# A retention layer and a swish MLP in one kernel: when TensorE gets the hosted batch's outputs and crosses, which PSUM bank its states take, and how the last rows are stored

## The chip, the cores and the metric

One core of one Trainium2 chip runs the kernel. The metric is the device time of the whole program in microseconds (us). The kernel before took 297.31 us, the median of three runs (296.36 to 298.05).

## The reference

Eight batches of eight heads (S = 576 positions, head width 64) go through a causal retention: scores of q and k, each multiplied by gamma(head) to the power of the distance, then multiplied by v. The result, 4608 rows of 512, goes through `g = h * sigmoid(beta * h)` with `h = x @ w_in` (512 to 2048), and `g @ w_out` (2048 to 512) is returned in float32.

```
ret = scale * (q @ k^T) * gamma ** (i - j)   for i >= j, else 0
x   = (ret @ v), heads side by side          # 4608 x 512
h   = x @ w_in ; g = h * sigmoid(beta * h)   # 4608 x 2048
out = g @ w_out                              # 4608 x 512
```

## The kernel before, in words

**Tiling.** Each batch's first 512 positions are one block of rows; the last 64 positions of all eight batches together are a ninth block. Blocks are counted 0 to 8 here. For every block, TensorE makes 16 "ups" (`up`, L702: four matmuls of 128x512 into one PSUM bank, which ScalarE then turns into `gT`), and then the second matrix product. Blocks 0 to 2 do that product directly (`down`, L806). From block 3 on it is done with seven products in the manner of Strassen (`seven_mm`, L739, in the order 3, 4, 1, 5, 2, 7, 6): each is 16 matmuls of 128x256, on the halves of `gT` itself or on sums of such halves (`seven_a`, L723, on VectorE), against combinations of w_out's quarters that were made before (`seven_b`, L248 and L244). In these blocks the odd rows of `gT` take two steps: ScalarE writes `hs` (L706) and VectorE scales it into `gT` (L707).

**The hosted batch.** While TensorE works at block n it also does the retention of batch b = n + 1, in small matmuls of 64x64, which run four at a time. Batch b's work has these steps: `scores` (sc and the second half of the batch's states, `four_states`), the folds (`fold`, L533 to L542: VectorE adds each of four partial states to a running sum, the fourth one at L537, and writes bf16 copies), four masks (L286, VectorE, from the scores in PSUM to `R`), `outputs4` (O<-R,vn, needs all four masks), a small copy on ScalarE that orders two kinds of matmul in one bank (`fence`, L505), and `crosses4` (O from q and the earlier states; for most batches also the first half of the next batch's states). Then O is copied into `xT`, the operand of the next block's ups (L625). In block 7 the ninth block's rows take the same place (`tail_scores`, `tail_outputs`, `tail_crosses`).

**PSUM.** Eight banks in rings by tag: `mm` (three: ups, the chains U and W, and one of the two banks of four states), `st` (one: the other bank of four states), `O` and `sc` (two each). A tile of a ring waits for the readers of the tile that held its bank. `state_banks` (L522) gives two banks for four partial states: those with index 0 and 1 lie in bank 0, those with 2 and 3 in bank 1, and `fold` reads them in this order. Before, bank 0 is `st` and bank 1 is `mm`.

**The order.** Nothing is scheduled by a tool: `fill` is TensorE's list (ups, downs, products), and `merged` (L826) puts other steps before the item at which they are due. In the lists `t = base[n]` is the first up of block n, so `t + 14` means ahead of its up 14, and `t + 16` ahead of its first product (two items for each product). All engines get their instructions in the order in which the steps are put, and each engine runs its own in that order. The lines that set the order here are L996 to L1002 (sums for the products) and L1005 to L1036 (hosted batch). For n = 3 (`SB`) outputs4 is due at t + 14 and crosses4 at t + 15; for n = 4, 5, 6 at t + 12 and t + 13; in block 7 at t + 13 and t + 14. In block 1 the second half of the scores is due 9.5 items ahead of block 2's first up, outputs4 4.2 items later and crosses4 one more.

**Loads and stores.** All large DMAs are issued by SP in the same order of steps: loads of q, k and v, transposes (L362), stores. GpSimd casts and scales q, k, v (L317, L328, L354). The products' results are gathered in `ot` and stored by `seven_store` (L768): after product 7 two rows of tiles, after product 6 the other two, 256 KB each.

Of the kernel before, what the change touches and what calls it, by code (L numbers as in the profile page):

```python
# [11 lines left out]
F32 = mybir.dt.float32  # L12
# [7 lines left out]
def kernel(  # L20
# [22 lines left out]
    TL = S - MB  # L43
# [6 lines left out]
    SB = 3  # L50
    KH = FO // 2
    NH = d_model // 2
# [13 lines left out]
    psum = ctx.enter_context(tc.psum_pool(name="psum", bufs=1))  # L66
# [218 lines left out]
    def F(f, *a):  # L285
        return lambda: f(*a)  # L286
# [232 lines left out]
        return [F(step, p, j ^ x) for p in range(HP) for j in range(2)]  # L519

    def state_banks():
        return [psum.tile([P, 2, HP, D], F32, name="st", tag=t, bufs=n) for t, n in (("st", 1), ("mm", 3))]  # L522
# [80 lines left out]
    def crosses4(b, later=None):  # L603
# [140 lines left out]
    def seven_out(m, j, ps, n):  # L744

        if m not in ots:
            ots[m] = stage.tile([P, MB // P, d_model], F32, name="ot", tag="ot", bufs=2)
        q = ots[m][:].rearrange("s (p a) (c n) -> s a c p n", a=2, c=2)
        c11, c12, c21, c22 = (q[:, a, c, ps] for a in range(2) for c in range(2))
        U, W, Z = (chains.get((c, n)) for c in "UWZ")  # L750
        if j == 4:
            nc.scalar.copy(c12, W[:])
            nc.vector.tensor_tensor(c21, c12, U[:], ALU.add)
        elif j == 1:
            nc.scalar.copy(c22, Z[:])
        elif j == 5:
            nc.scalar.copy(c11, W[:])
            nc.vector.tensor_tensor(c12, c21, c11, ALU.subtract)
        elif j == 2:
            nc.vector.tensor_tensor(c21, c21, U[:], ALU.subtract)  # L760
        elif j == 7:
            nc.vector.tensor_tensor(c11, c11, Z[:], ALU.add)
            seven_store(m, 0, ps)
        elif j == 6:
            nc.vector.tensor_tensor(c22, c22, U[:], ALU.add)
            seven_store(m, 1, ps)

    def seven_store(m, a, ps):  # L768

        for p in range(ps.start, ps.stop):  # L770
            if m < B:
                nc.sync.dma_start(out[m * S:m * S + MB].rearrange("(s i) n -> s i n", i=CB)[:, 2 * p + a], ots[m][:, 2 * p + a])
            else:
                rows = out.rearrange("(b s) n -> s b n", s=S)[MB + a * TL // 2:MB + (a + 1) * TL // 2, CB * p:CB * (p + 1)]
                nc.sync.dma_start(rows, ots[m][:, 2 * p + a])

    phs = {}

# [14 lines left out]
    pos_, ots, held = {}, {}, []  # L793
# [117 lines left out]
    base = {1: u1 + 10}  # L911
# [75 lines left out]
    def queued(at, steps):  # L987
        return [(x, lambda: steps.pop(0)()) for x in at]
# [7 lines left out]
    for n in range(SB, B + 1):  # L996
        t, m = base[n], blocks[n]
        first, second = slice(0, KH // 2), slice(KH // 2, KH)
        early = [t + 14.2, t + 14.9, t + 15.6, t + 15.8] if n == SB else [t + 9.6, t + 10.4, t + 11.2, t + 14.4] if n < B else span(t + 9, 4)
        streams.append([(x, F(seven_a, m, j, first)) for x, j in zip(early, (1, 5, 2, 7))] +  # L1000
                       [(t + 16.4 + 0.1 * x, F(seven_a, m, j, second)) for x, j in enumerate((1, 5, 2, 7))] +
                       [(t + 22.1, F(seven_a, m, 6))])  # L1002

    todo = list(range(2 * CB, len(seq), 2))
    for n in range(1, B):  # L1005

        take = [i for i in todo if seq[i][0] == n + 1 or n == B - 1]
        todo = todo[len(take):]
        b, t = n + 1, base[n]
        t0 = t + lead.get(n, 0)  # L1010
        if n == 1:
            at = [t + 17, base[b] - 9.5]
        elif n < SB:
            at = [t + 3, t + 18]
        else:
            at = [t0 - 13, t0 + 2] if n < B - 1 else [t0 - 9.5, t0 - 2.5]
        for i, x in zip(take, at, strict=True):
            streams.append(pair_prep(i, x))
        if n == 1:
            streams.append([(d0 + 6.1, F(mask, late, [1, CB], [CB, PC // 2])),  # L1020
                            (d0 + 6.2, F(mask, tri, [1, TL]))])
            streams.append([(at[0], F(group1, b, (0,))), (at[1], F(group1, b, (1,))), (at[1] + 4.2, F(outputs4, b)), (at[1] + 5.2, F(crosses4, b))])
        elif n < SB:
            streams.append([(t + 16, F(first_states, b))] * (b == XB + 1) +
                           [(t + 19, F(group1, b, (0, 1))), (t + 25, F(outputs4, b)), (t + 26, F(crosses4, b))])
        elif n == B - 1:
            outs = []
            streams.append([(t0, F(tail_scores, take[0])), (t + 13, F(tail_outputs, take[0])), (t + 14, F(tail_crosses, take[0], outs))] +
                           queued([t + 16.3, t + 17.6, t + 20.5, t + 22.5], outs))
        else:  # L1030
            rest, outs = [], []
            t0 -= behind[n]
            if b == SB + 2 and SB == XB + 1:
                streams.append([(t + 0.5, F(first_states, b))])
            streams.append([(t0, F(scores, b, (0, 1), rest))] + queued(span(t0 + 0.1, 4, 0.8) + span(t0 + 3.3, 4, 0.9), rest))
            streams.append([(t + (14 if n == SB else 12), F(outputs4, b)), (t + (15 if n == SB else 13), F(crosses4, b, outs))] + queued([t + 16.3] * 4 + [t + 17.3, t + 18.3, t + 20.3, t + 20.4][:0 if n in (SB, B - 2) else 4], outs))  # L1036
    assert not todo
    merged(fill, *streams)

# [29 lines left out]
```

## Time and profile before

| | |
|---|---|
| time, median of 3 runs | 297.31 us (296.36 to 298.05) |
| profiled execution: its time / its span | 297.5 us / 295.8 us |
| mean granted TensorE clock | 0.999 |
| HBM read / written | 36.71 MB / 9.44 MB, 156 GB/s over the span |
| ACT busy | 170.9 us (58%) |
| POOL busy | 123.3 us (42%) |
| DMA packets | 128309, 54.03 MB |

The span runs from the first to the last instruction; 1.7 us of the profiled time lie outside it. A TensorE matmul's record is longer than the time that it holds the engine, since matmuls are pipelined: the next one starts before the record ends. So time that TensorE lost is read here as the distance from one start to the next, less what the instruction between them usually takes. Times in a timeline row are: start, length (of a run of instructions, if xN is over 1), and in brackets the idle time before it and what ended it.

### The profile page before, as it was taken

How to read it: one execution, taken by the hardware profiler on the slowest of the kernel's cores; microseconds unless marked ns; L12 is line 12 of the kernel's file. 1: busy time of each engine (PE TensorE's matmuls, PEld its weight loads, DVE VectorE, ACT ScalarE, POOL GpSimd, SP SyncE). 2: the span in 40 equal slices, each digit the busy share in tenths (PEclk: the TensorE clock that was granted, in tenths of full speed). 3: DMA queues.
4: the chain of work that ended last, by engine and by line, in shares of the span. 5: the costliest groups of instructions: out<-in, count | busy, mean ns of one | idle time of the engine just before them, and what ended most of it. 6: DMA issues, size and time to landing. Idle time of an engine off the chain costs nothing.

```text
span 295.8 us, 8242 instructions
## 1 busy us (share of the span) xinstructions
PE 282.8 (96%) x3433; PEld 174.1 (59%) x3433; DVE 185.1 (63%) x341; ACT 170.9 (58%) x300; POOL 123.3 (42%) x219
## 2 busy tenths in 40 slices
PE   7799999999899999979999999899999999999994
PEld 5554446864444544437844685468547854784583
DVE  6563556704994395397579854987497645652672
ACT  5577556687858873655156734673376157737730
POOL 5666216673746381496447159245066200000000
PEclk9999999999999999999999999999999999999999
DMA  7999999998999999799798969955588530003003
GB/s 212 218 348 387 386 265 224 234 182 195 217 173 240 237 249 175 186 268 194 132 242 227 194 182 276 189 109 115 179 191 149 91 144 3 2 31 113 0 0 144
DMA packets 128309, 54.03 MB, mean 183 GB/s; under 512 B 110336, under 2 KB 120592, under 8 KB 128272
## 3 DMA queue, kind: packets, MB, share of 16 engines
q1 hardware_dynamic: 128240, 53.49, 78.7%
q8 instruction: 27, 0.44, 0.7%
q14 instruction: 10, 0.08, 0.1%
q10 hardware_dynamic: 32, 0.01, 0.0%
HBM read 36.71 MB, written 9.44 MB: 156 GB/s over the span
## 4 chain that ended last, share of the span: by engine, by line
PE 64%; SPq 14%; DMA 10%; DVE 8%; issue 1%; POOL 1%; ACT 1%; DVEq 0%; POOLq 0%
PE ph L702 27%; PE U L739 11%; SPq L100 8%; PE po L806 8%; PE W L739 7%; PE Z L739 7%; DMA wt<-in_moe_w_out_dram 3%; PE O L499 3%; DMA wt<-in_moe_w_in_dram 2%; DVE gT L707 2%; SPq L105 2%; DMA kvn<-in_v_dram 2%; DVE R L286 2%; PE sc L499 2%; SPq L86 1%; DMA kT<-kn 1%
## 5 line engine op out<-in xcount | busy, mean ns | idle before, releaser
L702 PE MATMUL ph<-xT,w_in_sb 128*128 128x512 bf16 (+1 forms) x560 | 118.7, 364 | 1.6 <-DVE end L537 1.4
L702 PEld LDWEIGHTS <-w_in_sb 128*128 128x128 bf16 x560 | 52.5, 98 | 57.0 <-DVE end L537 2.9
L709 ACT ACTIVATE gT<-ph,beta_sb 128x512 bf16<-128x512 f32 (+1 forms) x92 | 58.3, 641 | 46.6 <-PE ph L702 45.7
L354 POOL CAST kn<-kvn 128x128 bf16<-128x128 f32 (+2 forms) x80 | 32.8, 444 | 55.9 <-DMA kvn<-in_k_dram 55.6
L707 DVE TENSOR_SCALAR gT<-hs,ratio 128x512 bf16<-128x512 f32 x48 | 28.3, 589 | 35.4 <-ACT hs L706 35.1
L739 PEld LDWEIGHTS <-sa 128*128 128x128 bf16 x480 | 47.0, 98 | 5.4
L706 ACT ACTIVATE hs<-ph,beta_sb 128x512 f32<-128x512 f32 x48 | 33.0, 687 | 20.8 <-PE ph L702 20.5
L806 PE MATMUL po<-w_out_sb,gT 128*128 128x512 bf16 x192 | 43.8, 379 | 0.0
L723 DVE TENSOR_TENSOR sa<-gT 128x1024 bf16<-128x1024 bf16 (+1 forms) x54 | 41.5, 807 | 1.5 <-PE Z L739 1.3
L317 POOL TENSOR_TENSOR qs<-qn,gq 128x256 bf16<-128x256 f32 (+1 forms) x36 | 27.6, 792 | 23.4 <-issue 13.0
L328 POOL TENSOR_TENSOR vn<-kvn,gv 128x512 bf16<-128x512 f32 x32 | 34.6, 1090 | 4.4 <-DMA kvn<-in_v_dram 3.2
L806 PEld LDWEIGHTS <-gT 128*128 128x128 bf16 x192 | 17.9, 98 | 20.2
L739 PE MATMUL U<-b,sa 128*128 128x256 bf16 x192 | 22.9, 273 | 0.0
L739 PE MATMUL Z<-b,sa 128*128 128x256 bf16 x192 | 22.9, 273 | 0.0
L286 DVE TENSOR_TENSOR R<-sc,late 128x512 bf16<-128x512 f32 x24 | 15.3, 681 | 11.4 <-issue 10.2
L739 PEld LDWEIGHTS <-gT 128*128 128x128 bf16 x192 | 18.8, 98 | 3.4
L248 DVE TENSOR_TENSOR b<-wt 128x512 bf16<-128x512 f32 x20 | 15.2, 815 | 3.1 <-ACT wt L231 1.8
L407 DVE TENSOR_TENSOR R<-sc,causal 128x512 bf16<-128x512 f32 x16 | 10.2, 685 | 4.6 <-PE sc L403 4.5
L788 PE MATMUL ph<-xT,w_in_sb 128*128 128x512 bf16 x56 | 12.5, 379 | 0.2 <-ACT xT L460 0.2
L739 PE MATMUL U<-b,gT 128*128 128x256 bf16 x96 | 11.5, 273 | 0.0
L739 PE MATMUL W<-b,gT 128*128 128x256 bf16 x96 | 11.5, 273 | 0.0
L739 PE MATMUL W<-b,sa 128*128 128x256 bf16 x96 | 11.5, 273 | 0.0
(119 smaller groups left out, 288.5 us busy)
## 6 DMA issues: line engine op xcount, KB each, us to landing
out_dram<-ot SPq DMA_DIRECT2D x36, 256.0 KB, 3.3
qn<-in_q_dram SPq DMA_DIRECT2D x16, 512.0 KB, 5.5
kvn<-in_k_dram SPq DMA_DIRECT2D x20, 256.0 KB, 5.3
kvn<-in_v_dram SPq DMA_DIRECT2D x20, 256.0 KB, 5.3
wt<-in_moe_w_out_dram SPq DMA_DIRECT2D x8, 512.0 KB, 9.3
kvn<-in_k_dram SPq DMA_DIRECT2D x24, 128.0 KB, 3.6
kvn<-in_v_dram SPq DMA_DIRECT2D x24, 128.0 KB, 3.8
wt<-in_moe_w_in_dram SPq DMA_DIRECT2D x5, 512.0 KB, 8.4
```

The costliest lines, as they stand in the source:

```text
L100: nc.sync.dma_start(t[:, j], src[c * P:(c + 1) * P])
L286: return lambda: f(*a)
L317: nc.gpsimd.tensor_tensor(batch[b]["qs"][:, cs, to], q_tiles[b][:, hs, cs].rearrange("p h i d -> p i h d"), gq[:, cs, hs].unsqueeze(3).to_ ...
L328: nc.gpsimd.tensor_tensor(live[i]["vn"][:], kv_tiles.pop(i)[:, 1], gains(gv, row_of(b, c)), ALU.mult)
L354: nc.gpsimd.tensor_copy(kn[:, c % 2, to], t[:, 0, hs])
L702: nc.tensor.matmul(ph, w_in_sb[:, ko, fo * P:(fo + 1) * P], xts[m][:, ko, :, w], start=(ko == 0), stop=(ko == KO - 1))
L706: nc.scalar.activation(h, ph, ACT.Silu, scale=beta_sb[:, fo:fo + 1])
L707: nc.vector.tensor_scalar(gts[m][:, fo], h, ratio[:, fo // 2:fo // 2 + 1], None, ALU.mult)
L709: nc.scalar.activation(gts[m][:, fo, :, w], ph, ACT.Silu, scale=beta_sb[:, fo:fo + 1])
L723: nc.vector.tensor_tensor(sums_a[0][:, held_in[j], ks], quarter(m, *x, ks), quarter(m, *y, ks), op)
L739: nc.tensor.matmul(chains[c, n][:, 0 if alone else p], a, sevens[k // 2][:, j - 1, k % 2, :], start=j in (3, 4, 1) and k == 0 and (alone o ...
L806: nc.tensor.matmul(po[:, :nn], gT[:, fo, ms, :], w_out_sb[:, fo, n0:n0 + nn], start=(fo == 0), stop=(fo == FO - 1))
```

## The change

It does four things. Each engine keeps the computing instructions that it had; SP has four more stores.

1. `state_banks`: bank 0 of four partial states is now in `mm` and bank 1 in `st`.
2. `outputs4` and `crosses4` get other places: block 3, t + 14 / t + 15 becomes t + 15.3 / t + 17.3 (all 16 ups first, then outputs, product 3, crosses); block 4, t + 12 / t + 13 becomes t + 13 / t + 15.2 (crosses behind all ups); blocks 5 and 6, outputs at t + 10 (two ups sooner), crosses still at t + 13; block 7, outputs two ups sooner; block 2, crosses one item later. In block 1 the second half of the scores comes one item later, outputs stay where they were, and crosses come one item later. Copies of O queued for block 3 come two items later.
3. `seven_a`: in block 3 the sums are put in the order of the products that need them, both halves of the sum for products 1 and 5 ahead of those for 2 and 7; in block 4 the first halves are due at t + 11, 12, 14.4, 15.3 where they were due at t + 9.6, 10.4, 11.2, 14.4; in blocks 5 to 7 two due times move by 0.2 and 0.4, which changes no order on VectorE there.
4. `seven_store`: in the ninth block (m == B) each half row of tiles is stored as soon as its product has finished it, eight stores of 128 KB in place of four of 256 KB. In other blocks nothing changes.

```
-        return [... for t, n in (("st", 1), ("mm", 3))]
+        return [... for t, n in (("mm", 3), ("st", 1))]
...
+            done = (0, slice(NH, d_model))        # after product 5; likewise 2, 7, 6
...
+        if m == B and j in (5, 2, 7, 6):
+            seven_store(m, done[0], ps, done[1])
+        elif m < B and j in (7, 6):
+            seven_store(m, done[0], ps, slice(0, d_model))
...
+        if n == SB:
+            halves = [(t + 14.4, 1, first), (t + 15.1, 5, first), (t + 16.3, 1, second), (t + 16.4, 5, second)] + \
+                     [(t + 17.5 + 0.5 * x, j, ks) for x, (j, ks) in enumerate((j, ks) for j in (2, 7) for ks in (first, second))]
+        else:
+            early = [t + 11, t + 12, t + 14.4, t + 15.3] if n == SB + 1 else [t + 9.6, t + 10.6, t + 11.6, t + 14.4] if n < B else span(t + 9, 4)
...
-            at = [t + 17, base[b] - 9.5]
+            at = [t + 17, base[b] - 8.9]
...
-            ... (at[1] + 4.2, F(outputs4, b)), (at[1] + 5.2, F(crosses4, b))
+            ... (at[1] + 3.9, F(outputs4, b)), (at[1] + 5.9, F(crosses4, b))
...
-                           ... (t + 25, F(outputs4, b)), (t + 26, F(crosses4, b))
+                           ... (t + 25, F(outputs4, b)), (t + 27, F(crosses4, b))
...
-            ... (t + 13, F(tail_outputs, take[0])), (t + 14, F(tail_crosses, take[0], outs))
+            ... (t + 11, F(tail_outputs, take[0])), (t + 14, F(tail_crosses, take[0], outs))
...
-            streams.append([(t + (14 if n == SB else 12), F(outputs4, b)), (t + (15 if n == SB else 13), F(crosses4, b, outs))] + queued([t + 16.3] * 4 + ...
+            by = (t + 15.3, t + 17.3) if n == SB else (t + 13, t + 15.2) if n == SB + 1 else (t + 10, t + 13)
+            streams.append([(by[0], F(outputs4, b)), (by[1], F(crosses4, b, outs))] + queued([t + 16.3 + 2 * (n == SB)] * 4 + ...
```

More of the change, by code (lines that the diff above doesn't have):

```diff
@@ L521, in state_banks @@
     def state_banks():
-        return [psum.tile([P, 2, HP, D], F32, name="st", tag=t, bufs=n) for t, n in (("st", 1), ("mm", 3))]
+        return [psum.tile([P, 2, HP, D], F32, name="st", tag=t, bufs=n) for t, n in (("mm", 3), ("st", 1))]
     def four_states(b, e, bank):
@@ L998 @@
         first, second = slice(0, KH // 2), slice(KH // 2, KH)
-        early = [t + 14.2, t + 14.9, t + 15.6, t + 15.8] if n == SB else [t + 9.6, t + 10.4, t + 11.2, t + 14.4] if n < B else span(t + 9, 4)
-        streams.append([(x, F(seven_a, m, j, first)) for x, j in zip(early, (1, 5, 2, 7))] +
-                       [(t + 16.4 + 0.1 * x, F(seven_a, m, j, second)) for x, j in enumerate((1, 5, 2, 7))] +
+        if n == SB:
[3 more added lines that the diff above has]
+            early = [t + 11, t + 12, t + 14.4, t + 15.3] if n == SB + 1 else [t + 9.6, t + 10.6, t + 11.6, t + 14.4] if n < B else span(t + 9, 4)
+            halves = [(x, j, first) for x, j in zip(early, (1, 5, 2, 7))] + [(t + 16.4 + 0.1 * x, j, second) for x, j in enumerate((1, 5, 2, 7))]
+        streams.append([(x, F(seven_a, m, j, ks)) for x, j, ks in halves] +
                        [(t + 22.1, F(seven_a, m, 6))])
```

21 lines of the change are left out of this document (11 added, 10 removed).

## The prediction

> **What bounds the kernel now.** I read the page first (engine shares), then a table of the blocks, then the timeline of TensorE and VectorE in each block where TensorE stood.
>
> ```profile
> span 295.8 us, 8242 instructions
> PE 282.8 (96%) x3433; PEld 174.1 (59%) x3433; DVE 185.1 (63%) x341; ACT 170.9 (58%) x300; POOL 123.3 (42%) x219
> ```
>
> TensorE is the bound: busy for 96% of the span, where VectorE has 63% and the others less. The change adds and removes no matmul. So it can only gain time in which TensorE stands, and lose by making it stand elsewhere. From block 3 on, cut at each block's first up (length, then busy time of PE, PEld, DVE, ACT and POOL, granted clock, DMA share, GB/s):
>
> ```profile
> 116.50:147.90 31.40, 29.25 (x394) 19.16 (x393) 19.83 (x32) 15.46 (x25) 17.86 (x27) 1.00 0.92 195
> 147.90:178.70 30.80, 29.99 (x458) 19.52 (x456) 24.03 (x45) 16.10 (x28) 14.86 (x24) 1.00 0.89 214
> 178.70:208.70 30.00, 29.17 (x427) 19.13 (x426) 22.37 (x37) 16.10 (x28) 16.37 (x28) 1.00 0.82 159
> 208.70:237.30 28.60, 28.60 (x394) 18.93 (x392) 19.89 (x33) 14.88 (x24) 12.27 (x21) 1.00 0.72 158
> ```
>
> Blocks 3 to 6 have the same ups, products and nearly the same small matmuls, and take 31.4, 30.8, 30.0 and 28.6 us, all at a granted clock of 1.00. Block 6 shows no idle time, so it is what a block costs unhindered, and blocks 3, 4 and 5 have about 2.8, 2.2 and 1.4 us to give, 6.4 together. Now where they stand. The unit is an up in an unbroken run of block 8 (chain of waits, in order of time): 16 ups in 13.81 us, 0.863 each; an up ahead of small matmuls takes about 0.11 more.
>
> ```profile
> 265.77 13.81 PE ph L702 x64
> ```
>
> **Block 3.** TensorE, then VectorE:
>
> ```profile
> 123.71 5.50 PE L702 MATMUL ph<-xT,w_in_sb 128*128 128x512 bf16 x24
> 129.50 1.04 PE L702 MATMUL ph<-xT,w_in_sb 128*128 128x512 bf16 x4 [0.29 <-DVE end L537]
> 132.11 0.32 PE L499 MATMUL O<-R,vn 64*64 64x64 bf16 x17 [1.58 <-DVE R L286]
> 132.71 0.57 PE L499 MATMUL O<-R,vn 64*64 64x64 bf16 x47 [0.28 <-DVE R L286]
> 133.21 1.04 PE L702 MATMUL ph<-xT,w_in_sb 128*128 128x512 bf16 x4
> ```
> ```profile
> 126.96 0.41 DVE L535 TENSOR_TENSOR sum<-warm,st 128x256 f32<-128x256 f32 x1
> 129.03 0.41 DVE L537 TENSOR_TENSOR end<-sum,st 128x256 bf16<-128x256 f32 x1
> 130.79 1.87 DVE L286 TENSOR_TENSOR R<-sc,late 128x512 bf16<-128x512 f32 x3
> ```
>
> Ups 7 to 12 should end at 123.71 + 6 x 0.863 = 128.89; up 13 begins at 129.50, as the fourth fold (L537, ended 129.44) frees its bank. Then the outputs are due, and wait for the third mask (132.04) and, after 17 matmuls, for the fourth (130.79 + 1.87 = 132.66). They end at 133.21, and ups 14 and 15 follow.
>
> Swap: the `mm` bank is read by folds one and two alone, and is free at 126.96 + 0.41 = 127.37. That is 0.2 us behind the turn of up 11 (123.71 + 4 x 0.863 = 127.16), so about 0.4 of the 0.6 us goes. Move: ups 13, 14 and 15 end near 129.1 + 2.6 = 131.7 and the outputs wait from 131.8. VectorE works without a pause from the first fold to the last mask and waits for nothing that comes later than before, so the fourth mask still ends at 132.66 and the outputs at 133.21. But the two ups are done: **2 x 0.863 = 1.7 us gained**. The swap gives nothing of its own here, since the masks end the wait. Product 3 covers the crosses, which need only the fence on ScalarE. What is late next is VectorE's row of sums: their new order has the sum for product 1 ready first. The subtle one is the read of U (L753) behind all eight sums, ahead of product 2: counted from 132.66 at 0.7 to 0.8 a piece it ends 0 to 0.5 us ahead of that product. I take 0, and 0.3 as the worst.
>
> **Block 4.**
>
> ```profile
> 151.60 0.45 PE L499 MATMUL st<-vn,kn 64*64 64x64 bf16 x32
> 151.98 5.50 PE L702 MATMUL ph<-xT,w_in_sb 128*128 128x512 bf16 x24
> 157.77 2.76 PE L702 MATMUL ph<-xT,w_in_sb 128*128 128x512 bf16 x12 [0.29 <-DVE end L537]
> 163.58 3.07 PE L702 MATMUL ph<-xT,w_in_sb 128*128 128x512 bf16 x12
> 166.49 0.71 PE L739 MATMUL U<-b,gT 128*128 128x256 bf16 x5
> ```
> ```profile
> 151.29 0.42 DVE L535 TENSOR_TENSOR sum<-sum,st 128x256 f32<-128x256 f32 x1
> 159.32 1.87 DVE L286 TENSOR_TENSOR R<-sc,late 128x512 bf16<-128x512 f32 x3
> ```
>
> Without the bank wait up 9 begins at 151.98 + 5.18 = 157.16, and one up more fits ahead of the outputs: it ends at 160.6, when the masks (end 159.32 + 1.87 = 161.19) are still missing. So the outputs end as before 0.57 behind the fourth mask, as in block 3, at 161.8, and one up fewer is left to do then: 0.86 gained. Ups 13 to 15 took 166.49 - 163.58 = 2.91, 0.3 over three ups, waiting for the folds of the next batch's states. Behind the ups these states hold a bank that only block 5 asks for: 0.3 gained. Lost: the scores' states now need the `st` bank, which the fourth fold of the states before reads until 151.71, where they began at 151.60: 0.15. After the crosses the folds and sums stand in VectorE's queue ahead of product 1, with next to no room; 0 taken, 0.3 as the worst. **Block 4: 1.0 us.**
>
> **Blocks 5 and 6.**
>
> ```profile
> 180.60 5.50 PE L702 MATMUL ph<-xT,w_in_sb 128*128 128x512 bf16 x24
> 186.94 4.49 PE L702 MATMUL ph<-xT,w_in_sb 128*128 128x512 bf16 x20 [0.83 <-DVE end L537]
> 220.29 0.71 PE L499 MATMUL O<-R,vn 64*64 64x64 bf16 x64
> ```
> ```profile
> 183.25 0.94 DVE L542 CAST sbd<-warm 128x256 bf16<-128x256 f32 x1
> 184.12 0.41 DVE L535 TENSOR_TENSOR sum<-warm,st 128x256 f32<-128x256 f32 x1
> 184.56 0.29 DVE L542 CAST sbd<-sum 128x256 bf16<-128x256 f32 x1
> 187.80 1.88 DVE L286 TENSOR_TENSOR R<-sc,late 128x512 bf16<-128x512 f32 x3
> 216.44 1.88 DVE L286 TENSOR_TENSOR R<-sc,late 128x512 bf16<-128x512 f32 x3
> ```
>
> In block 5 the bank wait is 186.94 - (180.60 + 5.18) = 1.16 us. The swap removes most of it (the second fold ends at 184.53). But the outputs now come behind up 9, near 180.60 + 9 x 0.863 + 0.6 = 189.0, and the masks end at 187.80 + 1.88 = 189.68: TensorE waits there for what it waited for before. Outputs end near 190.25, three ups later it is 192.84, and the crosses follow at 192.95. Before, the outputs came at 186.94 + 5 x 0.863 + 0.11 = 191.36, and with 0.6 for them and one up the crosses at 192.9. **Gain 0.** Bounds: all of 1.16 if VectorE's run is shorter, minus the same if longer. In block 6 the outputs move two ups, from 220.29 to 218.56, and the masks end at 216.44 + 1.88 = 218.32: 0, with 0.24 us of room. In block 7 TensorE's work is unbroken and its masks are done five ups ahead: 0.
>
> **Blocks 1 and 2.**
>
> ```profile
> 74.51 0.45 PE L499 MATMUL sc<-qT,kT 64*64 64x64 bf16 x32 [0.47 <-DMA kT<-kn]
> 85.42 0.81 PE L702 MATMUL ph<-xT,w_in_sb 128*128 128x512 bf16 x3
> ```
> ```profile
> 78.47 2.56 ACT L231 ACTIVATE wt<-wt,rbeta_sb 128x512 f32<-128x512 f32 x4
> 81.49 0.69 DVE L813 COPY ot<-po 128x512 f32<-128x512 f32 x1
> 82.11 1.29 DVE L625 CAST xT<-O 128x512 bf16<-128x512 f32 x2
> ```
>
> One more down ahead of the scores hides the wait for kT (0.47 by the row, 0.6 as the next start shows it). But a copy of a down (0.69) then stands ahead of the masks on VectorE, so ScalarE's four L231, which end at 78.47 + 2.56 = 81.03, end near 81.65, and the fence behind them lets the crosses go no sooner than before: VectorE's two xT copies still begin near 82.1 to 82.3. From the first of them to block 2's first up it was 85.42 - 82.11 = 3.3 us, and in it stand now both of ScalarE's L244 ahead of its own xT copies. I take 0, and the 0.6 of one copy to both sides. Block 2's crosses come one down later, with four downs of block 2 left behind them to cover the copies: 0.
>
> **The end.**
>
> ```profile
> 290.00:296.00 6.00, 1.81 (x17) 1.37 (x15) 1.26 (x3) 0.00 (x0) 0.00 (x0) 0.94 0.47 175
> out_dram<-ot SPq DMA_DIRECT2D x36, 256.0 KB, 3.3
> ```
>
> The four last stores (1 MB) kept the DMA engines busy for 0.47 x 6 = 2.8 us, 0.70 each; the last one, of 128 KB, needs half: 0.35 gained. The lower bound is 0, if the 3.3 us that a store takes to land do not follow its size. Four more issues on SP, which has nothing else there, fit between products. **0.35.**
>
> **Sum**: 1.7 + 1.0 + 0 + 0 + 0.35 = 3.05 us off the profiled execution's 297.5 us (span 295.8, 1.7 around it): 294.45. The median of the runs shown is 0.2 lower, so I say **294.4**.
>
> **Rivals.**
>
> *GpSimd's run slides into VectorE's.* GpSimd is fed by loads that do not follow TensorE; by block 5 VectorE is 2.7 us earlier against it.
>
> ```profile
> 178.65 3.33 POOL L317 TENSOR_TENSOR qs<-qn,gq 128x256 bf16<-128x256 f32 x5 [0.48 <-DMA qn<-in_q_dram]
> 184.97 1.04 POOL L328 TENSOR_TENSOR vn<-kvn,gv 128x512 bf16<-128x512 f32 x1
> ```
>
> From the one to the other GpSimd hardly pauses, and works to 186.0, and two of block 5's casts took 0.94 where the third took 0.29. Earlier by 2.7 us, all three casts and the gT scalings fall into it: two or three more meetings at 0.65, less what overlaps, 0.9 in block 5 and 0.4 in block 4: 297.5 - 3.05 + 1.3 = 295.75. Against: GpSimd idles ahead of 178.65, so VectorE also leaves some. The Trainium skill, "SBUF — State Buffer", section "Who interferes with whom", says that of the two engines the one that starts first holds their shared port pair for its whole instruction and the other blocks; the pairs 0.94 and 0.29 agree, and by it a longer mask run is to be had in every block, 295.75. Chance 0.20.
>
> *Slower: the outputs outrun the masks.* Outputs two ups sooner in blocks 5 and 6 pay every microsecond of a longer mask run one for one. If half of the six casts and scalings of a run each wait out a GpSimd step of about 0.8 (3.33 / 5 = 0.67 to 1.04), block 5 loses 2.4 and block 6 2.4 less 0.24, 4.6 in all: 299.1. It is slower from a stretch of 4.55 us on. For it: the 0.94; against: in block 6 GpSimd is busy for only 12.27 of 28.6 us (the table of the blocks), and its loads there stand behind block 5's stores and so come earlier with it. Chance 0.11.
>
> *The feed is the bound*, and the change's gain is waited away at the next scores.
>
> ```profile
> 144.89 1.26 SPq L362 DMA_TRANSPOSE kT<-kn  x1
> ```
>
> The transpose for block 4 takes to 144.89 + 1.26 = 146.15; the scores that read kT run just ahead of 151.60 and would now run 1.7 sooner, 3.7 us behind it. If the feed slips by some 4 us, blocks 3 and 4 lose 1.7: 296.2. For it: the wait of 0.47 for kT in block 1. Chance 0.08.
>
> **How the numbers follow.** Forecast 0.61, rivals 0.20, 0.11, 0.08. This measurement tells 0.5% (1.5 us: below 295.8, above 298.8) from no change. Faster: nearly all of the first and half of the second, 0.69; slower 0.11; same 0.20. The range takes in the terms' bounds (1.2 us of gain at most: block 5 or block 1) and the first and third rivals: 293.2 to 297.0; left out are the slower case and the edges, under 0.2.
>
> **What would show it.** Block 3: no up between the outputs and product 3, outputs' second part ended by the fourth mask, the block near 29.7 us long. Block 4: no TensorE wait for L537, about 29.8 us. Block 5: the wait moves from L537 to L286 ahead of the outputs, 30 us. Block 2's first up near 85.4. Last stores of 128 KB. Wrong would be: outputs of block 6 that wait for masks by more than 0.5 us, a wait for kT in block 4, or block 2 beginning over 0.6 us later.

## The result, and the profile after

The changed kernel took **293.99 us**, the median of six runs (293.45 to 294.68), against 297.78 (296.36 to 299.94) for the kernel before in the same rounds: ratio 0.9864, 95% interval 0.9820 to 0.9908. In a second set of rounds (e12 below) it took 294.56, ratio 0.9888 (0.9845 to 0.9932). The forecast was 294.4.

The page of the changed kernel; its columns are those of the page before:

```profile
span 292.1 us, 8226 instructions
PE 280.0 (96%) x3401; PEld 174.1 (60%) x3433; DVE 185.9 (64%) x341; ACT 171.0 (59%) x300; POOL 123.9 (42%) x219
```

The span is 3.7 us shorter and the work is the same. TensorE shows 3401 matmuls for 3433 because 32 records are missing in this trace. Where the first matmul of a block is among them, the block's start is taken one matmul (0.22 us) earlier below.

Distances between the blocks' first ups, in us, from the traces of before, of the changed kernel and of its second run (e12). Block 1 is counted from the up that follows its last small matmuls (at 56.14, 56.10 and 56.84), and block 8 reaches to the end of the span. The cuts are the starts of the ups themselves, so the column of before differs by up to 0.07 from the prediction's rows, whose cuts were rounded:

| block | before | changed | changed again | forecast of the gain |
|---|---|---|---|---|
| 1 (its last part) | 29.28 | 28.99 | 29.37 | 0 |
| 2 | 31.11 | 31.16 | 31.17 | 0 |
| 3 | 31.33 | 29.97 | 29.70 | 1.7 |
| 4 | 30.86 | 29.94 | 29.94 | 1.0 |
| 5 | 29.97 | 29.38 | 29.96 | 0 |
| 6 | 28.62 | 28.62 | 28.60 | 0 |
| 7 | 28.30 | 28.30 | 28.30 | 0 |
| 8 and the end | 30.18 | 29.64 | 29.60 | 0.35 |

The table of blocks 3 to 6 by windows (length, busy time of PE, PEld, DVE, ACT and POOL, clock, DMA share, GB/s), first for the changed kernel, then for its second run:

```profile
116.25:146.22 29.97, 29.11 (x392) 19.12 (x392) 20.51 (x32) 15.50 (x25) 16.28 (x26) 1.00 0.94 195
146.22:176.16 29.94, 29.56 (x455) 19.55 (x456) 23.82 (x45) 16.23 (x28) 14.10 (x24) 1.00 0.88 189
176.16:205.54 29.38, 28.89 (x422) 19.43 (x424) 22.28 (x37) 16.12 (x28) 14.43 (x24) 1.00 0.95 203
205.54:234.16 28.62, 28.41 (x390) 19.02 (x393) 20.41 (x33) 14.89 (x24) 15.55 (x27) 1.00 0.71 160
```
```profile
117.38:147.08 29.70, 29.02 (x393) 19.11 (x392) 19.50 (x32) 15.49 (x25) 16.54 (x27) 1.00 0.98 201
147.08:177.02 29.94, 29.89 (x459) 19.81 (x457) 23.80 (x45) 16.23 (x28) 13.14 (x22) 1.00 0.77 189
177.02:206.98 29.96, 29.27 (x427) 19.32 (x425) 20.75 (x37) 16.12 (x28) 15.42 (x25) 1.00 0.90 190
```

The rows add up to 3.65 and 3.01 us; the second trace came to the last part of block 1 0.70 us late. The gains of blocks 3 and 4 and of the end are in both traces; that of block 5 is in one of them only.

**Block 3**, TensorE, VectorE and GpSimd in the timeline of the changed kernel:

```profile
123.50 8.21 PE L702 MATMUL ph<-xT,w_in_sb 128*128 128x512 bf16 x35
132.21 0.32 PE L499 MATMUL O<-R,vn 64*64 64x64 bf16 x17 [0.51 <-DVE R L286]
132.81 0.57 PE L499 MATMUL O<-R,vn 64*64 64x64 bf16 x47 [0.28 <-DVE R L286]
```
```profile
126.14 0.68 DVE L542 CAST sbd<-warm 128x256 bf16<-128x256 f32 x1
127.19 0.60 DVE L542 CAST sbd<-sum 128x256 bf16<-128x256 f32 x1
128.15 0.29 DVE L542 CAST sbq<-sum 128x256 bf16<-128x256 f32 x1
128.36 1.27 DVE L707 TENSOR_SCALAR gT<-hs,ratio 128x512 bf16<-128x512 f32 x1
130.88 1.87 DVE L286 TENSOR_TENSOR R<-sc,late 128x512 bf16<-128x512 f32 x3
```
```profile
125.57 1.10 POOL L317 TENSOR_TENSOR qs<-qn,gq 128x512 bf16<-128x512 f32 x1 [3.97 <-DMA qn<-in_q_dram]
127.03 3.65 POOL L317 TENSOR_TENSOR qs<-qn,gq 128x256 bf16<-128x256 f32 x5 [0.35 <-DMA qn<-in_q_dram]
```

All nine ups stand in one run from 123.50 (35 of their 36 matmuls are in the trace), and no up is left between the outputs and the products. The outputs still wait for the third and the fourth mask. The fourth ends at 130.88 + 1.87 = 132.75, 0.1 us later than before although the block began 0.28 sooner. The reason is in the other rows: two casts and one scaling of gT took 0.68, 0.60 and 1.27 us where 0.29 and 0.48 are the least, and GpSimd's scaling of q lies beside all three. In the trace of before, one cast took 0.68 and two scalings 0.84 and 0.90.

**Block 4 and block 5**, TensorE:

```profile
149.97 0.60 PE L499 MATMUL st<-vn,kn 64*64 64x64 bf16 x32
154.43 5.35 PE L702 MATMUL ph<-xT,w_in_sb 128*128 128x512 bf16 x24 [0.22 <-DVE sum L535]
159.72 0.71 PE L499 MATMUL O<-R,vn 64*64 64x64 bf16 x64
```
```profile
186.06 0.32 PE L499 MATMUL O<-R,vn 64*64 64x64 bf16 x17
186.65 0.57 PE L499 MATMUL O<-R,vn 64*64 64x64 bf16 x47 [0.28 <-DVE R L286]
```

In block 4 no up waits for the fourth fold (L537) any more; one waits for the second (L535), and the outputs run without a pause. The states behind the scores take 0.60 where they took 0.45: they wait for the `st` bank, the 0.15 that was set down for it. In the second trace they take 0.82 and no up waits. In block 5 the wait has moved from L537 ahead of the ups to the last mask ahead of the outputs.

**The end**: the last VectorE step of the kernel before, then of the changed one:

```profile
291.85 0.42 DVE L765 TENSOR_TENSOR ot<-ot,U 128x256 f32<-128x256 f32 x1 [0.45 <-PE U L739]
```
```profile
288.70 0.42 DVE L767 TENSOR_TENSOR ot<-ot,U 128x256 f32<-128x256 f32 x1 [0.45 <-PE U L739]
```

From the end of that step to the end of the span it was 295.79 - 292.27 = 3.52 us, and is 292.10 - 289.12 = 2.98. SP now issues eight stores, from 283.44 on.

### The profile page after: what moved, and what is told of

It reads as the page before. It is cut to its first block, busy times and chain, and to the rows that moved or that the text cites. A ratio compares the mean times of both kernels' runs of the same rounds, so it can differ in the third digit from the quotient of the medians.

```text
span 292.1 us, 8226 instructions
## 1 busy us (share of the span) xinstructions
PE 280.0 (96%) x3401; PEld 174.1 (60%) x3433; DVE 185.9 (64%) x341; ACT 171.0 (59%) x300; POOL 123.9 (42%) x219
## 4 chain that ended last, share of the span: by engine, by line
PE 64%; SPq 10%; DVE 8%; DMA 8%; POOL 3%; issue 3%; ACT 2%; DVEq 0%; ACTq 0%
PE ph L702 28%; PE U L739 11%; SPq L100 8%; PE W L739 7%; PE Z L739 7%; PE po L812 6%; DMA wt<-in_moe_w_out_dram 3%; PE O L499 3%; DVE R L286 2%; DMA qn<-in_q_dram 2%; DMA wt<-in_moe_w_in_dram 2%; DVE gT L707 2%; ACT wt L231 2%; PE sc L499 1%; SPq L86 1%
## 5 line engine op out<-in xcount | busy, mean ns | idle before, releaser
L702 PE MATMUL ph<-xT,w_in_sb 128*128 128x512 bf16 (+1 forms) x540 | 115.9, 364 | 1.3 <-DVE sum L535 0.2
L354 POOL CAST kn<-kvn 128x128 bf16<-128x128 f32 (+2 forms) x80 | 33.9, 458 | 56.2 <-DMA kvn<-in_k_dram 55.8
L723 DVE TENSOR_TENSOR sa<-gT 128x1024 bf16<-128x1024 bf16 (+1 forms) x54 | 42.8, 830 | 1.5 <-PE Z L739 1.3
L812 PE MATMUL po<-w_out_sb,gT 128*128 128x512 bf16 x182 | 42.3, 379 | 1.2 <-issue 1.0
L286 DVE TENSOR_TENSOR R<-sc,late 128x512 bf16<-128x512 f32 x24 | 15.3, 679 | 11.4 <-issue 10.2
L248 DVE TENSOR_TENSOR b<-wt 128x512 bf16<-128x512 f32 x20 | 15.3, 817 | 3.3 <-ACT wt L231 1.8
L625 ACT CAST xT<-O 128x512 bf16<-128x512 f32 x19 | 9.8, 597 | 4.7 <-PE O L499 4.7
```

The costliest lines, as they stand in the source:

```text
L354: nc.gpsimd.tensor_copy(kn[:, c % 2, to], t[:, 0, hs])
L702: nc.tensor.matmul(ph, w_in_sb[:, ko, fo * P:(fo + 1) * P], xts[m][:, ko, :, w], start=(ko == 0), stop=(ko == KO - 1))
L723: nc.vector.tensor_tensor(sums_a[0][:, held_in[j], ks], quarter(m, *x, ks), quarter(m, *y, ks), op)
L812: nc.tensor.matmul(po[:, :nn], gT[:, fo, ms, :], w_out_sb[:, fo, n0:n0 + nn], start=(fo == 0), stop=(fo == FO - 1))
```

## The experiments

Three theories stand against each other. A is the forecast: each edit acts in its own block, and a freed wait pays only where nothing else is late next. B says that the swap of the banks carries most of it. C is the forecast's first rival: the length of VectorE's run from the first fold to the fourth mask follows what GpSimd does beside it. Ratios are to the kernel before in the same rounds.

| run | median us | ratio (95%) | blocks 3, 4, 5 |
|---|---|---|---|
| e1 | 296.96 | 0.9985 (0.9948 to 1.0021) | 32.40, 31.01, 29.14 |
| e2 | 295.32 | 0.9923 (0.9895 to 0.9951) | 30.40, 29.94, 29.95 |
| e3 | 295.89 | 0.9944 (0.9913 to 0.9974) | 30.13, 31.08, 30.03 |
| e4 | 297.23 | 0.9986 (0.9957 to 1.0015) | 31.07, 31.92, 28.97 |
| e5 | 292.27 | 0.9813 (0.9754 to 0.9873) | 28.60, 29.53, 28.97 |
| e6 | 294.49 | 0.9893 (0.9840 to 0.9946) | 30.58, 30.47, 29.65 |
| e7 | 294.21 | 0.9888 (0.9832 to 0.9945) | 30.51, 29.54, 29.59 |
| e8 | 294.56 | 0.9884 (0.9835 to 0.9933) | 29.99, 30.29, 29.31 |
| e9 | 293.07 | 0.9845 (0.9805 to 0.9884) | 29.08, 29.84, 29.57 |
| e10 | 299.40 | 1.0067 (1.0033 to 1.0102) | 31.25, 33.25, 28.93 |
| e11 | 298.90 | 1.0034 (1.0000 to 1.0068) | 34.32, 31.72, 28.90 |
| e12 | 294.56 | 0.9888 (0.9845 to 0.9932) | 29.70, 29.94, 29.96 |

**e1, the swap alone** (on the kernel before):

```
-(("st", 1), ("mm", 3))
+(("mm", 3), ("st", 1))
```

> The kernel before with the two banks of four partial states swapped and nothing else. Theory A (a freed wait pays only where nothing else is late next): block 3 gains 0, since the outputs wait for the masks there; block 4 gains 0 at the outputs for the same reason and 0.3 us at the three ups behind the crosses; block 5 gains the whole wait of 1.0 us, since its outputs come two ups later than in the changed kernel, behind the masks. About 1.3 us of 297.5 in all, so 296.2. Rival B (the swap carries most of the change): 2.5 to 3 us, with blocks 3 and 4 shorter by about 1 us each. Rival C (the length of VectorE's run from folds to masks follows its overlap with GpSimd, not the waits): the blocks move by up to 0.5 us either way whatever the swap does.

Measured: 0.4 us, with an interval from 1.5 gained to 0.6 lost. B is out. The runs differ in their granted clock: four of the ten have a mean of 0.994 and took 297.16 to 299.53 us, the profiled one among them, and six have 1.000 and took 295.48 to 297.66, median 296.11. Of the 29 runs of the kernel before, 22 have 0.997 or more, median 297.32; against these the six gain 1.2 us, which is A's size. TensorE in block 4, then in block 5:

```profile
154.81 0.41 PE L499 MATMUL st<-vn,kn 64*64 64x64 bf16 x26 [0.31 <-DVE sum L535]
155.97 0.23 PE L499 MATMUL st<-vn,kn 64*64 64x64 bf16 x5 [0.76 <-issue]
183.60 9.74 PE L702 MATMUL ph<-xT,w_in_sb 128*128 128x512 bf16 x44
```

Block 5 does what A says: 11 ups in one run, and 29.14 us for 29.97. But block 4 pays: the scores' states wait for the swapped bank and lose 1.4 us there in two pauses, the second of which the trace puts down to no semaphore, and the block takes 31.01 us for 30.86. The 32.40 of block 3 has a cause of its own (last section).

**e2, the swap undone** (in the changed kernel; the reverse of e1's edit).

> The changed kernel with the banks as they were before. Theory A: block 3 loses 0 to 0.1 us (the up that waits for the fourth fold then ends just ahead of the masks); block 4 loses 0.4 to 0.8 (an up waits for the fourth fold again and the outputs no longer wait for masks) and up to 0.3 behind the crosses; block 5 about 0 (the outputs wait for the masks either way). 0.5 to 1.2 us slower than the changed kernel, 294.5 to 295.2. Rival B (the swap carries most): 2 us or more slower, 296 and above.

Measured: 0.8 to 1.3 us slower than the two medians of the changed kernel, which were taken in other rounds. That is near A's size, and B's 2 us or more are out. The places are not A's. TensorE in block 3, then in block 4:

```profile
130.63 2.76 PE L702 MATMUL ph<-xT,w_in_sb 128*128 128x512 bf16 x12 [1.32 <-DVE end L537]
133.33 0.71 PE L499 MATMUL O<-R,vn 64*64 64x64 bf16 x64
```
```profile
156.83 3.63 PE L702 MATMUL ph<-xT,w_in_sb 128*128 128x512 bf16 x16 [0.32 <-DVE end L537]
```

In block 3 the wait for the fourth fold is back, 1.32 us, and the outputs then find their masks ready: 30.40 us for the block against 29.97 and 29.70. One wait had been traded for the other. VectorE's run was also the longest of all here, 7.36 us, and its fourth mask came 16.88 us behind the block's first up, for 16.50 and 16.24. In block 4 an up waits for that fold too, 0.32 us, but the outputs run without a pause and the scores' states do not wait: the block takes 29.94 us, as long as with the swap, where A had 0.4 to 0.8 lost. Block 5 takes 29.95 (29.38 and 29.96 with the swap) and block 6 28.85 (28.62 and 28.60).

**e3, block 3's part alone**, on the kernel before (with the changed kernel's order of block 3's sums and copies):

```
+by = (t + 15.3, t + 17.3) if n == SB else (t + 12, t + 13)
```

> The kernel before with block 3's part alone: outputs behind all ups, crosses behind product 3, copies and sums in the new order. Theory A: block 3 is 1.4 to 1.7 us shorter (two ups fill the wait for the masks), all other blocks as before within 0.1 at the ups; 295.9 of 297.5. Rival C (VectorE's overlap with GpSimd): blocks 4 and 5, which begin 1.4 us sooner against GpSimd's loads, change by up to 0.5 us each, though nothing in them was touched. Rival D (the sums come too late): products 1 or 2 of block 3 wait and the gain is under 1 us.

Measured: 1.7 us (0.8 to 2.6) by the times, 1.2 in the trace's block 3, and blocks 4 and 5 as before within 0.25. A holds, a little short of its 1.4 to 1.7 in the trace: as in e2, up 13 waits 1.33 us for the fourth fold, and the outputs then wait for no mask. No product waits for a sum, so D is out.

**e4, block 4's part alone**, on the kernel before:

```
+by = (t + 14, t + 15) if n == SB else (t + 13, t + 15.2) if n == SB + 1 else (t + 12, t + 13)
+early = ... else [t + 11, t + 12, t + 14.4, t + 15.3] if n == SB + 1 else [t + 9.6, t + 10.4, t + 11.2, t + 14.4] ...
```

> The kernel before with block 4's part alone: outputs one up later, crosses and the next batch's states behind all ups, first halves of the sums later. Theory A: the outputs still end with the masks and one up fewer follows, 0.86 us, and 0.3 us of the ups that waited for the folds of the next states: block 4 about 1.1 us shorter, 296.4. Rival B (without the swap the wait of 0.45 us for the fourth fold takes the place of the gain): 0.4 us or less. Rival C: block 5 changes by up to 0.5 us too.

Measured: 0.4 us (1.3 gained to 0.4 lost), which is the size that B gave for this edit. The trace's block 4 is even 1.1 us longer. TensorE, VectorE and GpSimd in it:

```profile
158.22 3.63 PE L702 MATMUL ph<-xT,w_in_sb 128*128 128x512 bf16 x16 [1.08 <-DVE end L537]
```
```profile
154.29 1.18 DVE L542 CAST sbd<-warm 128x256 bf16<-128x256 f32 x1
156.49 0.94 DVE L542 CAST sbq<-sum 128x256 bf16<-128x256 f32 x1
```
```profile
153.26 1.06 POOL L354 CAST kn<-kvn 128x256 bf16<-128x256 f32 x3
154.28 1.04 POOL L328 TENSOR_TENSOR vn<-kvn,gv 128x512 bf16<-128x512 f32 x1
```

GpSimd came 2.7 us sooner in the block than in the trace of before, so that its k and v steps, not its q steps, lay beside the folds; two casts took 1.18 and 0.94, and the fourth fold came late. Without the swap an up waits for that fold, 1.08 us. But the missing swap alone does not explain it: e2 has the same places without the swap, and its block 4 is 0.92 us shorter than before. What differs by the traces is the company that the folds had, so theory C enters. Block 5 speaks for it as well: there GpSimd was done with q 0.2 us ahead of the block, VectorE's steps from the first fold to the fourth mask took 5.58 us for 6.87 before, and the block is 1.0 us shorter, though none of its places was changed.

**e5 and e6, the scaling of q left out** for batches 5, 6 and 7, in the changed kernel and in the kernel before (the scores of these batches are then of batch 4's q):

```
+if b in (SB + 2, SB + 3, SB + 4):
+    if n == 0:
+        batch[b] = dict(qs=batch[b - 1]["qs"], qT=...)
+    return
```

> The changed kernel without GpSimd's scaling of q (L317) for batches 5, 6 and 7, which runs beside blocks 3 to 5: those batches' transposes read the scaled q of batch 4 again, so their scores are of the wrong q. Nothing else is left out. Theory C (VectorE's 14 steps from folds to the fourth mask take 5.57 us with no GpSimd step of that kind beside them, as in block 6, and 6.3 to 7.4 us with it): the runs of blocks 3, 4 and 5, of 7.06, 6.58 and 6.33 us in the changed kernel, come down to 5.6 to 6.1. Block 3 gains the wait at its outputs, 0.9 to 1.1 us; block 4 the 0.4 us of the up that waits for the second fold; block 5 the 0.46 us ahead of its last mask: 1.5 to 2 us in all, 292.0 to 292.5. Rival E (the length is VectorE's own and its pauses are waits for ScalarE or TensorE): the runs stay within 0.2 us and so does the time.

> The kernel before with the same scaling left out. Theory C: its waits behind the same runs (6.75, 7.01 and 6.87 us) shrink: block 3 by 0.8 to 1.2 us, block 4 by 0.9 to 1.2, block 5 by 0.7 to 1.0, so 2.4 to 3.4 us off 297.5: about as much as the whole change brought. Theory A as it stands in the forecast (waits moved under other work) has nothing against that, but then the change on top of it, this run against e5, is worth less than the 3.7 us that the two profiles showed: 2 to 2.5. Rival E: 0 and 3.7.

Two VectorE steps in block 3 of e5 (its line numbers are four higher there), then blocks 3 to 5 of e5 by windows, then of e6:

```profile
125.95 0.29 DVE L546 CAST sbd<-warm 128x256 bf16<-128x256 f32 x1
127.48 0.48 DVE L711 TENSOR_SCALAR gT<-hs,ratio 128x512 bf16<-128x512 f32 x1
```
```profile
116.21:144.81 28.60, 28.60 (x393) 19.01 (x392) 19.30 (x32) 15.49 (x25) 12.46 (x21) 1.00 0.99 201
144.81:174.34 29.53, 29.53 (x458) 19.62 (x456) 23.11 (x45) 16.22 (x28) 10.44 (x17) 1.00 0.94 189
174.34:203.31 28.97, 28.97 (x426) 19.35 (x424) 20.55 (x37) 16.11 (x28) 9.94 (x16) 1.00 0.96 195
```
```profile
116.20:146.78 30.58, 29.05 (x393) 19.20 (x392) 17.53 (x32) 15.47 (x25) 11.58 (x21) 1.00 0.89 195
146.78:177.25 30.47, 29.62 (x458) 19.46 (x456) 22.80 (x45) 16.11 (x28) 8.46 (x17) 1.00 0.95 185
177.25:206.90 29.65, 29.14 (x427) 19.10 (x424) 21.10 (x37) 16.11 (x28) 9.83 (x18) 1.00 1.00 199
```

C holds and E is out. In e5 VectorE's runs from the first fold to the fourth mask (13 steps, not 14) took 5.57, 5.78 and 5.71 us in blocks 3 to 5 where the changed kernel had 7.06, 6.58 and 6.33; TensorE has no idle time left in these blocks, and the time is 292.27. Leaving out the scaling changes more than VectorE's company, but the lengths of single steps say the same in all fourteen traces: in these runs of blocks 3 to 6, the 70 casts with no GpSimd instruction beside them took 0.29 or 0.30 us and the 33 scalings of gT 0.47 or 0.48, while beside GpSimd casts took up to 1.18 and scalings up to 1.27.

The kernel before gains 2.8 us from the same omission, by the medians (297.27 before in these rounds). The change on top of it is worth 294.49 - 292.27 = 2.2 us, inside the 2 to 2.5 that C gave. Block by block C had too much: in e6's trace, the slowest of its four runs (295.81), blocks 3 to 5 gain 0.75, 0.39 and 0.32 us where 2.4 to 3.4 in all were expected. Block 5's run still took 6.54 us there, beside k's and v's steps, and TensorE met other waits, for masks in block 3 (0.86 us) and for a fold of the next states in block 4 (0.85).

**e7, outputs behind product 3** in block 3 (in the changed kernel):

```
-by = (t + 15.3, t + 17.3) if n == SB
+by = (t + 17.3, t + 19.3) if n == SB
-queued([t + 16.3 + 2 * (n == SB)] * 4
+queued([t + 16.3 + 4 * (n == SB)] * 4
```

> The changed kernel with block 3's outputs behind product 3 and its crosses behind product 4, copies two items later still. If the 1.1 us that TensorE waits there for the third and fourth mask are the end of that row, about 1.0 us is gained: 293.0. If VectorE's sums, which stand behind the masks in its queue, are late next (product 1 would begin near 136.4 where its last sum ends at 136.5 now, and the product after it needs the next sum at 137.1), 0.5 to 0.9 of it goes to them. If the copies to xT come too late for block 4's first up, block 4 begins with a wait and nothing is gained.

No gain: 294.21. The wait for the masks is gone and another is there (TensorE, then ScalarE):

```profile
138.16 1.91 PE L739 MATMUL Z<-b,sa 128*128 128x256 bf16 x16 [0.69 <-ACT xT L625]
```
```profile
137.52 2.05 ACT L625 CAST xT<-O 128x512 bf16<-128x512 f32 x4
```

Product 1 writes a bank of O's ring, and waits for the first copy out of it. None of the three expectations had this one. A wait of 1.1 us for kT at the scores hid what was left of the gain in this block.

**e8, the outputs of blocks 5 and 6 two ups later**, as before:

```
-(t + 13, t + 15.2) if n == SB + 1 else (t + 10, t + 13)
+(t + 13, t + 15.2) if n == SB + 1 else (t + 12, t + 13)
```

> The changed kernel with the outputs of blocks 5 and 6 back where they were, two ups later. Theory A: in block 5 the 0.46 us that TensorE stands ahead of the fourth mask are gained, in block 6 nothing (its masks are done in time either way): 293.5, or 0.4 to 0.6 us shorter in the profile's block 5. The slower rival of the forecast (outputs that outrun the masks) has its price here too: it is the difference of blocks 5 and 6 between this run and the changed kernel, 0.5 us by the present row, up to 1.7 us where GpSimd's work falls wholly into the run. If the earlier outputs do pay: crosses or copies are late and block 5 gets longer.

```profile
176.92:206.23 29.31, 29.29 (x426) 19.42 (x424) 22.36 (x37) 16.11 (x28) 17.55 (x29) 1.00 0.85 175
```

Block 5 has no idle time in this row, and takes 29.31 us against 29.38 and 29.96; block 6 is unchanged and the time is that of the changed kernel. The earlier place costs nothing that can be measured here, and gives nothing. The size expected was 0.4 to 0.6; with one trace of 29.38 and one of 29.96 to compare with, it is not settled.

**e9, outputs behind product 3, crosses in the middle of product 4**:

```
-by = (t + 15.3, t + 17.3) if n == SB
+by = (t + 17.3, t + 18.3) if n == SB
-queued([t + 16.3 + 2 * (n == SB)] * 4
+queued(([t + 18.4] * 2 + [t + 19.4] * 2 if n == SB else [t + 16.3] * 4)
```

> The changed kernel with block 3's outputs behind product 3, as in e7, but the crosses in the middle of product 4, half a product (0.87 us) sooner than in e7, and two of the four copies to xT ahead of ScalarE's copy of W. In e7 product 1 stood 0.87 us, its first matmul 0.05 us behind the end of the first copy to xT (138.16 against 138.11). If that copy, which frees the bank that product 1 writes, was the cause, the wait goes and block 3 is 28.7 to 29.1 us long where the changed kernel had 29.97: 293.0. If VectorE's sums were the cause, product 1 begins no sooner against the end of the fourth mask (4.75 us behind it in e7) and the block stays at 29.4 or more.

```profile
137.04 1.91 PE L739 MATMUL Z<-b,sa 128*128 128x256 bf16 x16
138.79 1.91 PE L739 MATMUL W<-b,sa 128*128 128x256 bf16 x16
140.80 1.47 PE L739 MATMUL U<-b,sa 128*128 128x256 bf16 x12
```

Product 1 follows without a wait, 4.0 us behind the fourth mask (4.75 in e7), so the copy was the cause, not the sums. The next wait in line is product 2's: 140.80 - 138.79 is 2.01 where a product takes 1.745, 0.27 lost. Block 3 takes 29.08 us, and at **293.07** this is the fastest kernel that does all the work. Its interval overlaps that of the changed kernel beside it (e12), so the 1.5 us between their medians are not settled by the times; the 0.6 to 0.9 in block 3 are in the traces.

**e10, q loaded sooner** (in the changed kernel), and **e11**, this with e9's places and outputs of blocks 5 and 6 at t + 11:

```
+ask = at - (36 if b >= SB + 2 else 30)
-st += [(at - 30, F(load_q, b, (0,)))]
+st += [(ask, F(load_q, b, (0,)))]
...
-st += [(at - 30, F(load_q, b, (1,)))]
+st += [(ask, F(load_q, b, (1,)))]
```

> The changed kernel with SP's two loads of q for batches 5, 6 and 7 put six items sooner, which moves them ahead of one transpose of kT (and of one store for batch 5); nothing is left out. Theory C: GpSimd's scaling of q, which runs 9.2 to 14.4 us into block 3, beside VectorE's run at 9.4 to 16.5, comes 2 to 3.6 us sooner and half of it leaves that run; the run gets 0.4 to 0.9 us shorter there, 0.2 to 0.7 in block 4 and 0.2 to 0.6 in block 5, and the time 0.8 to 1.6 us: 292.4 to 293.2. Rival F (the feed): 1 MB of q ahead of the transposes delays kT, and the scores of blocks 3 to 5 wait for it: the same or slower, with waits for kT by the trace. Rival E: runs as long as before.

> Both of these together, and the outputs of blocks 5 and 6 one up later than in the changed kernel. If the gains are in different waits they add up but for block 3, where they share the wait for the masks: 292.0 to 292.6. If shorter mask runs make the later places needless, it is no better than e10 or e9 alone.

e10 is slower than the kernel before, e11 no faster. Part of that is the clock (last section): seven of e10's ten runs and six of e11's have a granted clock of 0.994 or less. The others took 297.43 to 298.17 and 296.75 to 297.47 us, against a median of 297.03 for the 15 of 19 runs of the kernel before with 0.997 or more: no gain there either, and some 3 us more than the changed kernel beside them (e12). TensorE in blocks 3 and 4 of e10, then VectorE and GpSimd behind the ups of block 4:

```profile
125.23 0.45 PE L499 MATMUL sc<-qT,kT 64*64 64x64 bf16 x32 [2.15 <-DMA kT<-kn]
...
171.68 1.49 PE L739 MATMUL Z<-b,sa 128*128 128x256 bf16 x12 [1.24 <-DVE sa L723]
...
175.76 1.91 PE L739 MATMUL U<-b,sa 128*128 128x256 bf16 x16 [0.86 <-DVE ot L753]
```
```profile
169.49 5.63 DVE L723 TENSOR_TENSOR sa<-gT 128x1024 bf16<-128x1024 bf16 x5
```
```profile
171.44 4.72 POOL L317 TENSOR_TENSOR qs<-qn,gq 128x256 bf16<-128x256 f32 x5 [0.37 <-DMA qn<-in_q_dram]
```

C's half came true: the runs took 6.21, 5.72 and 5.58 us, and block 5 went to 28.93. F's half came true as well: kT's transpose in block 3 took 6.0 us from its issue to its landing, where it took 3.2 in the changed kernel, and the scores wait 2.2 us for it. More was lost where none of the theories looked. The scores' states of block 4 wait 1.3 us for the `st` bank, and the q steps of the next batch moved beside the sums, of which five took 5.63 us (the changed kernel: 4.13 for five in block 3), so products 1 and 2 wait.

**e12, the changed kernel again.**

> The changed kernel once more, beside the three others on the same chip: what one trace differs from the next of the same kernel. Theory C: the times at which GpSimd's scaling of q begins, and with them the lengths of VectorE's runs in blocks 3 to 5, differ from trace to trace by some tenths of a us, and the lengths of these blocks with them; blocks 6 and 7, without such scaling, agree within 0.05 us.

As expected: q's scaling begins 0.3 to 0.9 us sooner against the starts of blocks 3 to 5 than in the first trace, the runs took 6.43, 6.39 and 6.46 us, and blocks 3 and 5 differ by 0.27 and 0.58 us from the first trace. Blocks 6 and 7 agree within 0.02. In block 5 an up waits for the second fold. VectorE, then TensorE:

```profile
180.73 0.93 DVE L707 TENSOR_SCALAR gT<-hs,ratio 128x512 bf16<-128x512 f32 x1 [2.83 <-ACT hs L706]
```
```profile
183.10 4.49 PE L702 MATMUL ph<-xT,w_in_sb 128*128 128x512 bf16 x20 [0.46 <-DVE sum L535]
```

The scaling of gT just ahead of the folds, beside q's steps, took 0.93 us here and 0.49 in the first trace, so the whole run began 0.4 us later. In block 3 the same step took 0.99 and 0.48.

## Why the prediction was right

The time and its sign came out as forecast, and so did the blocks that gained in both traces. That 294.4 lies so near 293.99 is in part luck: the terms were off by up to 0.6 us and their errors partly cancel, 3.65 and 3.01 us in the two traces against a sum of 3.05. The last step of that sum is also off: 294.45 less 0.2 is 294.25, not 294.4. The terms one by one:

**Block 3** (1.7): 1.36 and 1.63. The two ups were done while the masks were missing, and the outputs still ended with the fourth mask. The gain fell short of two ups (1.73) by what the fourth mask came later, counted from the block's first up: 16.50 and 16.24 us for 16.13. In one trace the run grew, 7.06 us for 6.75; in the other it took 6.43 but began 0.4 us later, behind a longer scaling. The step "VectorE works without a pause, so the fourth mask still ends at 132.66" left out that its steps have no fixed length. The swap gives block 3 nothing of its own to speak of, as stated (e1, e2).

**Block 4** (1.0): 0.92 in both traces, but by another sum. The 0.15 for the states was there in the first trace, and 0.37 in the second. A wait for the second fold (0.4 us with the distance to the next start), which stood nowhere in the working for this block, took part of it in the first trace; against that the run was 0.43 and 0.62 us shorter, so the outputs waited for no mask at all. The working gave the swap a part in this block; e2 gains the same 0.92 without it.

**Block 5** (0): 0.59 and 0.01. The wait moved to the masks, as forecast. The run was shorter in both traces (6.33 and 6.46 us for 6.87), inside the bounds given; what differs is where it ended. The fourth mask came 10.44 us behind the block's first up in one trace and, behind the longer scaling, 11.02 in the other. The two blocks differ by the same 0.58.

**Blocks 6 and 7** (0): 0. **Blocks 1 and 2** (0, with 0.6 to both sides): in block 1 0.29 and -0.09, which is less than traces of kernels with the same block 1 differ by (28.47 to 29.94 in those that have it as before); block 2 -0.05.

**The end** (0.35): 0.54 and 0.58, mis-sized. All nine traces with eight stores of 128 KB have 29.60 to 29.68 us for block 8 and the end, all five with four of 256 KB have 30.16 to 30.18. The term took the engines' busy share for the whole cost of a smaller store. Where a trace has the last store's landing, it is 2.06 to 2.09 us behind the issue with 128 KB (seven traces) and 2.38 with 256 KB (e3 and e6): some 0.3, near the 0.35. From the landing to the end of the span it is 0.85 us for 1.10, and what this quarter of a microsecond is stays open.

**The rivals.** GpSimd's overlap is real and is what the blocks 3 to 5 still lose, but the first rival had its sign wrong in two blocks of three: coming sooner against GpSimd made the runs of blocks 4 and 5 shorter, since more of q's steps now lay beside them where k's and v's had, and in block 5 the casts of 0.94 went. The rule of the Trainium skill, "SBUF — State Buffer", section "Who interferes with whom", that GpSimd and a VectorE instruction which takes the port pair they share lock each other out for whole instructions, agrees with e5: with no GpSimd instruction beside them the casts take 0.29 and the scalings 0.48 us. Not every step is held up: the folds (0.41) and masks (0.68), which read one of their two sources from PSUM, took the same beside GpSimd as without it in all fourteen traces. The slower rival did not occur. The feed was not the bound in the changed kernel: in neither of its traces do the scores of blocks 3 to 5 wait for kT. But it is near: they waited 0.9 us in e7's trace, and 2.2 after one change in SP's order (e10).

One step of the working was wrong without harm to the sum. Blocks 3, 4 and 5 were said to have 2.8, 2.2 and 1.4 us to give against block 6's 28.6. In e5, with no idle time left, they take 28.60, 29.53 and 28.97, because blocks 4 and 5 have more small matmuls (x458 and x426 for x393). So they had 2.7, 1.3 and 1.0, and the change took 1.4 to 1.6, 0.9 and 0 to 0.6 of it.

## What to carry to other kernels

When one engine waits at the end of another's queue, move its own ready work in front of the wait before trying to shorten that queue; then look which buffer the moved work frees later (e7's bank cost the whole gain until the crosses moved too). A step's length on VectorE is not a constant where GpSimd works beside it: compare the same run of steps with and without that company before counting on its end. And an earlier load is not free in a queue that works in order: e10 got the shorter runs it was made for, and lost more to the transpose behind the load and to the steps that GpSimd's work now lay beside.

## What the runs showed of the hardware

In two traces TensorE's granted clock fell to half for a few microseconds in block 3. In e1 it did so right after the outputs had waited 2.4 us for their masks, and in e11 while the scores waited 2.9 us for kT. In the trace of before TensorE stood 2.2 us at e1's place and in that of e10 2.2 us at e11's, and the clock stayed. The rows of the two windows, e1 and then e11:

```profile
134.40:139.00 4.60, 4.60 (x81) 2.37 (x72) 1.96 (x2) 1.34 (x3) 1.68 (x4) 0.63 1.31 191
```
```profile
125.24:132.07 6.83, 5.93 (x76) 2.74 (x77) 2.21 (x5) 1.38 (x2) 5.88 (x12) 0.50 1.26 272
```

The clock was 0.50 from 134.61 to 138.02 in e1. At 0.63 of full speed its 4.6 us hold the work of 2.9, so 1.7 of the block's 32.40 us are the clock's. In e11 TensorE was busy for 5.9 us at half speed, so about 3 of the block's 34.32 us are the clock's.

The mean granted clock of the single runs shows it too. It is 0.994 or less in 12 of the 55 runs of the kernel before in the experiments' rounds, in 4 of 10 of e1, 7 of 10 of e10 and 6 of 10 of e11, and 0.998 or more in all ten runs of the changed kernel. A wait can thus cost more than its own length; that the waits set the fall off is what the two traces suggest, and no experiment here tested it.
